# Keeping a group's split weights in DRAM, and finer-grained row splits, in a fused attention, MoE and feed-forward kernel

## The chip, the cores and the metric

The kernel runs on one core of a Trainium2 chip. The metric is the device time of one execution in microseconds. Before the change the median of 3 runs is 956.89 us (955.63 to 957.21).

## The reference

Three layers in float32, 1,792 rows of 768. Sigmoid attention over 4 x 12 heads, a mixture of 8 experts of which each row uses its best one, and a dense gated feed-forward layer. The change lies in the last:

```python
def _moe2_ref(x, w_gate, w_val, w_out):          # 1792 x 768, 768 x 1536 (twice), 1536 x 768
    gate = 1.0 / (1.0 + np.exp(-(x @ w_gate)))
    val = x @ w_val
    return (gate * val @ w_out).astype(np.float32)
```

## The kernel before, in words

Attention comes first, then the experts (to about 468 us), then the feed-forward layer. Only the last is described.

It works in two row blocks, sb = 0 and 1, of 896 rows, and each in two stages. `gv_stage` (L1517) makes gate times value in 12 groups g: 6 tiles of features, for each a gate group (g even) and a value group (g odd). A group is one Strassen-Winograd product of 2 x 2 blocks: 7 products of sums of weight blocks and sums of row blocks. `o_stage` (L1655) multiplies by w_out the same way, 7 products for each of 3 (block 0) or 4 (block 1) pairs of row tiles.

For TensorE (PE) each operand x is split: hi = x rounded to fp32r, lo = x - hi, and a product is hi·hi + lo·hi + hi·lo: in `product` (L1420) three matmuls for each of 3 slices, so 9 matmuls of 128 x 448 in `gv_stage`, and 18 of 128 x 384 in `o_stage`. The hi part is a cast on ScalarE (ACT), the lo part a subtraction on VectorE (DVE).

- Rows: `y_load` brings a tile of expert output (yd, in DRAM) by a DMA from POOL; `y_turn` (L1303) transposes it on PE and copies it into YB. `y_sum` makes T1 to T4, `y_split` (L1356) splits a block. The lo part of B11, B21, B22 or T1 (`yl`) takes the place of that block itself in YB.
- Weights: `ff_load` fetches a group's raw blocks from wd by a DMA from SP into one of three buffers wr. `w_sums` (L1401, DVE, four instructions) makes S1 to S4; `w_hi` (ACT, L1413) and `w_lo` (DVE, L1418) split in two halves: blocks 0 to 2 (1152 columns) and 3 to 6 (1536 columns), into `wh` (two buffers, in turn) and `wl` (in place of wr).
- Some raw weights lie packed in DRAM and are unpacked by `decode` (DVE, L236 to L242, three steps).
- Output stage: `t_split` splits w_out's blocks (th, tl), loaded by `o_load` into q; `s_prep` (L1616) splits the squares of gate times value (sr).

PE's program order within a group is the order of the products; `gv_first` starts the next group's A11·B11 before this group's last two products. All other work is placed by hand between products: behind product n of a group, `hooks(n)` issues work on ACT, DVE and SP (n = 0 to 3 behind the first four, 4 behind `gv_first` of the next group, 5 and 6 behind S4·B22 and A22·T4). In `o_stage` `o_hooks(n, j)` does so behind product n of pair j. Each engine runs its instructions in the order of issue, so an instruction that waits holds everything behind it on that engine. Results leave PSUM by `out(k, ...)` on DVE (gate groups: t0g; value groups: G) and by copies on ACT: s, u (t0u, t1u), v (t0v, t1v). An operand's name tells block and part: y0B22hi is block 0, B22, hi part.

```python
        for n, f in enumerate(((p6, p2, p5, p7) if sb else (p6, p7, p5, p2)) if last else
                              (p2, p7, p6, p5) if (sb, g) == (1, 0) else (p7, p6, p2, p5)):
            f()
            if n < 3:
                hooks(n)
        out(3, d, u4)
        hooks(3)
```

The last two row tiles of the output leave by a direct DMA on SP, the others by an indirect one on POOL (`store`, L1646).

## Time and profile before

| | us |
|---|---|
| median of 3 runs | 956.89 |
| the profiled execution | 956.68 |
| its span | 954.6 |
| PE busy | 928.1 (97%) |
| DVE busy | 737.4 (77%) |
| ACT busy | 544.8 (57%) |
| POOL busy | 147.9 (15%) |
| feed-forward part, first matmul of block 0 | 468.69 |
| first matmul of block 1 | 702.88 |
| end of the last sum on DVE | 950.84 |

Matmuls are pipelined: a row of the timeline gives a matmul's start and its duration, and one begins every 0.20 us (128 x 448) or 0.17 us (128 x 384) while each lasts 0.36 or 0.33. In square brackets stands the time that the engine sat idle before, and the operation that ended it. SPq and POOLq are DMA issues. PEclk is the granted clock of PE as a share of its higher level.

### The profile page before, as it was taken

How to read it: one execution, taken by the hardware profiler on the slowest of the kernel's cores; microseconds unless marked ns; L12 is line 12 of the kernel's file. 1: busy time of each engine (PE TensorE's matmuls, PEld its weight loads, DVE VectorE, ACT ScalarE, POOL GpSimd, SP SyncE). 2: the span in 40 equal slices, each digit the busy share in tenths (PEclk: the TensorE clock that was granted, in tenths of full speed). 3: DMA queues.
4: the chain of work that ended last, by engine and by line, in shares of the span. 5: the costliest groups of instructions: out<-in, count | busy, mean ns of one | idle time of the engine just before them, and what ended most of it. 6: DMA issues, size and time to landing. Idle time of an engine off the chain costs nothing.

```text
span 954.6 us, 14878 instructions
## 1 busy us (share of the span) xinstructions
PE 928.1 (97%) x5757; PEld 781.6 (82%) x5757; DVE 737.4 (77%) x912; ACT 544.8 (57%) x645; POOL 147.9 (15%) x124
## 2 busy tenths in 40 slices
PE   9999999998999999999999999989999999999998
PEld 4555556887887887889978999989988999999998
DVE  6867767988998876799959888676997666658674
ACT  6586766576766666779643344355664343445451
POOL 0011112233052222324400000000220000000011
PEclk9999999999999999999989999999999999999999
DMA  8999967455899998766406554264231111125112
GB/s 300 336 341 340 331 209 276 155 179 186 301 406 420 313 331 336 260 238 199 149 1 215 181 173 159 94 251 152 83 116 67 56 47 65 67 100 199 50 50 83
DMA packets 36974, 186.40 MB, mean 195 GB/s; under 512 B 4680, under 2 KB 6744, under 8 KB 32800
## 3 DMA queue, kind: packets, MB, share of 16 engines
q1 hardware_dynamic: 25680, 134.29, 40.1%
q0 software_dynamic: 11216, 51.09, 14.2%
q8 instruction: 46, 0.75, 0.3%
q14 instruction: 32, 0.26, 0.1%
HBM read 180.94 MB, written 35.88 MB: 227 GB/s over the span
## 4 chain that ended last, share of the span: by engine, by line
PE 68%; DMA 2%; DVE 2%; ACT 2%; issue 1%; ACTq 0%; DVEq 0%
PE pb L1424 15%; PE pb L1425 15%; PE pb L1423 15%; PE h L1104 8%; PE y L1088 3%; PE y L1090 3%; PE y L1089 3%; DMA Y<-yd 2%; PE qh L1193 2%; PE qy L1216 1%; PE hTp L1123 1%; DMA yd<-yo,ridx 1%; PE xTp L950 1%; DVE tl L1586 1%; PE yTp L1313 1%
## 5 line engine op out<-in xcount | busy, mean ns | idle before, releaser
L281 DVE TENSOR_TENSOR rg<-raw,rg 128x1536 fp32r<-128x1536 f32 x104 | 179.9, 1752 | 32.0 <-ACT rg L280 26.6
L280 ACT CAST rg<-raw 128x1536 fp32r<-128x1536 f32 x102 | 150.4, 1480 | 59.1 <-PE y L1089 29.0
L1424 PE MATMUL pb<-yl,wh 128*128 128x448 f32 x288 | 105.7, 367 | 2.2 <-DVE yl L1359 2.2
L1104 PE MATMUL h<-rg,xh 128*128 128x512 f32 x336 | 102.2, 398 | 0.3 <-ACT rg L280 0.3
L1425 PE MATMUL pb<-th,sr 128*128 128x384 f32 x294 | 98.4, 335 | 1.4 <-DVE sr L1625 1.4
L1423 PE MATMUL pb<-th,sr 128*128 128x384 f32 x294 | 98.9, 336 | 0.0
L1424 PE MATMUL pb<-tl,sr 128*128 128x384 f32 x294 | 98.4, 335 | 0.2 <-DVE tl L1586 0.2
L436 ACT ACTIVATE attn<-sc,bias_s 128x896 f32<-128x896 f32 x84 | 79.1, 1004 | 28.3 <-PE sc L434 28.0
L1418 DVE TENSOR_TENSOR wl<-wr,wh 128x1536 fp32r<-128x1536 f32 (+1 forms) x43 | 67.9, 1580 | 16.1 <-ACT wh L1413 13.7
L1104 PEld LDWEIGHTS h<-rg,xh 128*128 128x128 f32 x336 | 61.2, 188 | 15.1 <-issue 1.6
L448 PE MATMUL av<-attn,v 128*64 128x448 f32 (+1 forms) x384 | 70.6, 545 | 0.6 <-DVE xT L453 0.5
L1088 PE MATMUL y<-rg,hh 128*128 128x384 f32 x192 | 67.1, 349 | 1.5 <-DVEq L1247 1.5
L1413 ACT CAST wh<-wr 128x1536 fp32r<-128x1536 f32 (+1 forms) x43 | 57.3, 1333 | 18.4 <-PE pb L1424 14.3
L1090 PE MATMUL y<-rg,hh 128*128 128x384 f32 x192 | 65.4, 341 | 1.2 <-DVE rg L281 1.2
L1089 PE MATMUL y<-rg,hl 128*128 128x384 f32 x192 | 65.4, 341 | 0.9 <-DVE hl L1129 0.8
L1104 PE MATMUL h<-rg,xl 128*128 128x512 f32 x168 | 61.5, 393 | 0.0
L1424 PEld LDWEIGHTS pb<-yl,wh 128*128 128x128 f32 x288 | 54.2, 188 | 7.3 <-DVE yl L1359 3.0
L1652 POOL DMA_INDIRECT out<-o,idc x12 | 17.5, 1458 | 271.4 <-ACT o L1670 227.6
L1425 PEld LDWEIGHTS pb<-th,sr 128*128 128x128 f32 x294 | 55.2, 188 | 1.7 <-DVE sr L1625 1.7
L1424 PEld LDWEIGHTS pb<-tl,sr 128*128 128x128 f32 x294 | 55.2, 188 | 0.6 <-DVE tl L1586 0.6
L1423 PEld LDWEIGHTS pb<-th,sr 128*128 128x128 f32 x294 | 55.2, 188 | 0.0
L1623 ACT CAST sr<-G 128x768 fp32r<-128x768 f32 x42 | 35.1, 838 | 30.4 <-PE pb L1424 18.9
(499 smaller groups left out, 2108.3 us busy)
## 6 DMA issues: line engine op xcount, KB each, us to landing
raw<-in_w1P SPq DMA_DIRECT2D x52, 768.0 KB
raw<-in_w2P SPq DMA_DIRECT2D x52, 768.0 KB
q<-wob SPq DMA_DIRECT2D x14, 1152.0 KB
wr<-wd SPq DMA_DIRECT2D x19, 768.0 KB
sg<-in_wffP SPq DMA_DIRECT2D x9, 1536.0 KB
kq<-in_kqP SPq DMA_DIRECT2D x24, 448.0 KB
stg<-in_wffP SPq DMA_DIRECT2D x5, 1536.0 KB
Y<-yd POOLq DMA_DIRECT2D x14, 384.0 KB, 6.5
```

The lines of the kernel that those rows point to most:

```text
L280: (hi_eng.tensor_copy if hi_eng else A.copy)(hi, raw)
L281: V.tensor_sub(lo, raw, hi)
L436: A.activation(at_, ps[:, :, :S], AF.Sigmoid, bias=bias_s, scale=1.0 / math.sqrt(HD))
L448: T.matmul(av_t[j * HD : (j + 1) * HD, i % 2, :S], v[rows, j * HD : (j + 1) * HD], at_[rows, j, :], start=(u == first_unit(i)), stop=(u == ...
L1088: T.matmul(o, ah[:, ks], bh[:, w], start=(k == 0), stop=False)
L1089: T.matmul(o, al[:, ks], bh[:, w], start=False, stop=False)
L1090: T.matmul(o, ah[:, ks], bl[:, w], start=False, stop=(k == nk - 1))
L1104: T.matmul(ps[:, half, :], x[:, k * P : (k + 1) * P], w[:, s * 512 : (s + 1) * 512], start=(k == 0 and x is xh and w is hi), stop=(k == KD ...
L1418: V.tensor_sub(w_los(g, half), raw, w_his(sb, g, half))
L1423: T.matmul(o, ah[:, k], bh[:, k], start=(first and k == 0), stop=False, skip_group_check=open_)
L1424: T.matmul(o, ah[:, k], bl[:, k], start=False, stop=False, skip_group_check=open_)
L1425: T.matmul(o, al[:, k], bh[:, k], start=False, stop=(k == n - 1), skip_group_check=open_)
```

## The change

1. A buffer `wkeep` in DRAM. The split weights of group (0, 0) go there by four DMAs from POOL (`w_keep`); block 1 fetches them with four DMAs from SP (`w_kept`) in place of loading raw weights, summing and splitting them again. Their hi part lies in a buffer of its own (`whk`).
2. YB becomes four buffers, yb00 to yb11. A turned tile is copied in two instructions everywhere.
3. In the first group of both blocks the casts of B22 and T4 stand at hooks 0 and 1, their subtractions at hooks 1 and 2 (before: both at 3 and 4). T1 of block 1 is split at hook 0 (before 1), T2 of block 0 one step earlier.
4. The scaling of the last expert pair stands earlier, in two halves.
5. The list of PSUM banks is rotated by two.
6. Block 1's first group runs p2, p6, p7, p5. `out(3)` follows as soon as p5 and p7 are both done.
7. In the second group the unpacking stands at hooks 2, 4, 6 (before 4, 5, 6). In block 1 `s_prep(1, 0)` stands at hook 2 of the last group (before 5). The first two turns of rows in block 0's output stage come one product later: (0, 2) and (1, 0).
8. The last row tile's store goes in two halves.

```diff
-    def y_split(sb, name):
+    def y_split(sb, name, parts=(0, 1)):
         hi, lo = buf(f"y{sb}{name}hi", y_place(sb, name + "hi"), KH, TH, dt=F32R), y_lo(sb, name)
-        A.copy(hi, y_raw(sb, name))
-        V.tensor_sub(lo, y_raw(sb, name), hi)
+        if 0 in parts:
+            A.copy(hi, y_raw(sb, name))
+        if 1 in parts:
+            V.tensor_sub(lo, y_raw(sb, name), hi)
...
     def y_block(kh, th):
-        return YB[:, kh, th]
+        return buf(f"yb{kh}{th}", (SB_Y, (2 * kh + th) * YA), KH, TH)
...
+    def w_keep():
+        for half, (a, b) in enumerate(HALVES):
+            for k, z in enumerate((w_his(0, 0, half), w_los(0, half))):
+                G.dma_start(wkeep[:, k, a * YW : b * YW], z.bitcast(U32))
+
+    def w_kept(half, ks=(0, 1)):
+        a, b = HALVES[half]
+        for k in ks:
+            z = w_los(0, half) if k else w_his(1, 0, half)
+            SP.dma_start(z.bitcast(U32), wkeep[:, k, a * YW : b * YW])
...
+        elif (sb, g) == (1, 0):
+            products = (p2, p6, p7, p5)
+        done = []
+        for n, f in enumerate(products):
             f()
-            if n < 3:
-                hooks(n)
-        out(3, d, u4)
-        hooks(3)
+            done.append(f)
+            if f in (p5, p7) and p5 in done and p7 in done:
+                out(3, d, u4)
+            hooks(n)
...
                 if g == 0:
-                    y = {1: sb and "T1", 3: "B22", 4: "T4"}.get(at_)
-                    if y:
-                        y_split(sb, y)
+                    if at_ == 0 and sb:
+                        y_split(sb, "T1")
+                    if at_ < 2:
+                        y_split(sb, ("B22", "T4")[at_], (0,))
...
+                    if g == 0 and at_ in (1, 2):
+                        y_split(sb, ("B22", "T4")[at_ - 1], (1,))
...
+                    if at_ == 5 - 3 * sb:
+                        s_prep(sb, 0)
                     if at_ - 1 - 2 * sb in (0, 1):
                         t_split(sb, 0, at_ - 1 - 2 * sb)
-                    elif at_ == 5:
-                        s_prep(sb, 0)
...
-                if dec is not None and at_ >= 4:
-                    decode(dec, at_ - 4)
+                when = (2, 4, 6) if g == 1 else (4, 5, 6)
+                if dec is not None and at_ in when:
+                    decode(dec, when.index(at_))
...
-                    if n in (4, 6):
+                    if sb and j == 3 and n > 4:
+                        h = int(n == 5)
+                        SP.dma_start(out[N - P :, h * 384 : (h + 1) * 384], o[:, h])
+                    elif n in (4, 6):
                         store(sb, q if n == 4 else r, o)
...
-    O_TURNS = {(0, 1): 0, (0, 2): 1, (1, 1): 2, (1, 2): 3, (2, 0): 4, (2, 1): 5, (2, 2): 6}
+    O_TURNS = {(0, 2): 0, (1, 0): 1, (1, 1): 2, (1, 2): 3, (2, 0): 4, (2, 1): 5, (2, 2): 6}
...
         if (n, j) == (4, 2):
-            ff_load(0)
+            w_kept(0)
+            w_kept(1, (1,))
         elif (n, j) == (5, 2):
             ff_load(1)
             ff_load(2)
-            w_sums(1, 0, 0)
         elif (n, j) == (6, 0):
             y_split(1, "B11")
-            w_sums(1, 0, 1)
         elif (n, j) == (6, 1):
-            w_hi(1, 0, 0)
-            w_lo(1, 0, 0)
+            w_kept(1, (0,))
             y_split(1, "B21")
         elif (n, j) == (6, 2):
             y_split(1, "T3")
-            w_hi(1, 0, 1)
-            w_lo(1, 0, 1)
...
+        if c == NW2 - 1:
+            y_scale(NSTAT - 1, 2)
         ff_first(c)
+    w_keep()
...
-    one_bank += [pbp.tile([P, 512], F32, name=f"pb{i}") for i in range(8)]
+    banks = [pbp.tile([P, 512], F32, name=f"pb{i}") for i in range(8)]
+    one_bank += banks[2:] + banks[:2]
```

ACT at the start of block 0, before, from the copy t0s of group 0 (wh is the next group's weights, t0g a gate):

```order
L1448 COPY t0s<-pb_6095 128x448
L1413 CAST wh_6129<-wr_5880 128x1152
L1483 COPY t0u_6114<-pb_6095 128x448
L1491 COPY t0v<-pb_6095 128x448
L1465 ACTIVATE t0g_6116<-t0g_6116 128x448
L1358 CAST y0B22hi<-YB 128x1344
L1413 CAST wh_6129<-wr_5880 128x1536
L1465 ACTIVATE t0g_6119<-t0g_6119 128x448
L1448 COPY t0s<-pb_6096 128x448
L1358 CAST y0T4hi<-y0T_5763 128x1344
```

The same place in the changed kernel:

```order
L1464 COPY t0s<-pb_6114 128x448
L1360 CAST y0B22hi<-yb_5456 128x1344
L1418 CAST wh_6149<-wr_5892 128x1152
L1499 COPY t0u_6131<-pb_6114 128x448
L1360 CAST y0T4hi<-y0T_5775 128x1344
L1507 COPY t0v<-pb_6114 128x448
L1481 ACTIVATE t0g_6133<-t0g_6133 128x448
L1418 CAST wh_6149<-wr_5892 128x1536
```

The casts of B22 and T4 have moved ahead of the copies t0u and t0v, which wait for products of PE.

DVE at the start of block 1, before, from the first sum o of the last pair (o are sums of the output stage, L1405 to L1409 weight sums, wl weight splits):

```order
L1672 TENSOR_TENSOR o_1_7303<-pb_6100,U_7245 128x384
L1359 TENSOR_TENSOR y1T3lo<-y1T_7495,y1T3hi 128x1344
L1418 TENSOR_TENSOR wl_1_6066<-wr_5878,wh_6045 128x1536
L1359 TENSOR_TENSOR y1T2lo<-y1T_7570,y1T2hi 128x1344
L1464 TENSOR_TENSOR t1g_7763<-pb_6097,t1s 128x448
L1405 TENSOR_TENSOR wr_5880<-wr_5880 128x384
L1406 TENSOR_TENSOR wr_5880<-wr_5880 128x384
L1359 TENSOR_TENSOR yl_5938<-YB,y1T1hi 128x1344
L1408 TENSOR_TENSOR wr_5880<-wr_5880 128x384
L1409 TENSOR_TENSOR wr_5880<-wr_5880 128x384
L1418 TENSOR_TENSOR wl_0_6145<-wr_5880,wh_6129 128x1152
L1464 TENSOR_TENSOR t1g_7766<-pb_6099,t1v 128x448
```

In the changed kernel:

```order
L1698 TENSOR_TENSOR o_1_7321<-pb_6119,U_7254 128x384
L1362 TENSOR_TENSOR y1T3lo<-y1T_7513,y1T3hi 128x1344
L1362 TENSOR_TENSOR y1T2lo<-y1T_7588,y1T2hi 128x1344
L1480 TENSOR_TENSOR t1g_7776<-pb_6116,t1s 128x448
L1362 TENSOR_TENSOR yl_5950<-yb_5454,y1T1hi 128x1344
L1410 TENSOR_TENSOR wr_5892<-wr_5892 128x384
L1411 TENSOR_TENSOR wr_5892<-wr_5892 128x384
L1413 TENSOR_TENSOR wr_5892<-wr_5892 128x384
L1414 TENSOR_TENSOR wr_5892<-wr_5892 128x384
L1423 TENSOR_TENSOR wl_0_6168<-wr_5892,wh_6149 128x1152
L1362 TENSOR_TENSOR yl_6147<-yb_5456,y1B22hi 128x1344
L1362 TENSOR_TENSOR y1T4lo<-y1T_7640,y1T4hi 128x1344
```

The weight split wl_1 of group 0 is gone from between T3 and T2 (the other half and the sums, earlier, too), and B22 and T4 stand ahead of the gate sum that waits for t1v.

SP's queue at the end of block 0's output stage, before the change only loads of raw weights, with it:

```order
L1601 DMA q_7176<-wob_78 128x2304
L1434 DMA wh_7612<-wkeep 128x1152
L1434 DMA wl_0_6059<-wkeep 128x1152
L1434 DMA wl_1_6082<-wkeep 128x1536
L1324 DMA wr_5892<-wd_65 128x1536
L1324 DMA wr_6061<-wd_66 128x1536
L1434 DMA wh_6239<-wkeep 128x1536
L1324 DMA wr_5890<-wd_67 128x1536
```

Three loads of kept parts stand where one raw load (of wd_64) stood, and the fourth behind the raw loads of groups 1 and 2.

## Rows read from the trace of the kernel before

**Rows 1.** The page, busy time of each engine.

```profile
PE 928.1 (97%) x5757; PEld 781.6 (82%) x5757; DVE 737.4 (77%) x912; ACT 544.8 (57%) x645; POOL 147.9 (15%) x124
```

**Rows 2.** Timeline of PE, block 0's first two groups: start, duration, operation.

```profile
477.97 0.36 PE L1423 MATMUL pb<-y0B11hi,wh 128*128 128x448 f32 x1
...
480.49 0.47 PE L1423 MATMUL pb<-y0B22hi,wh 128*128 128x448 f32 x1 [0.53 <-ACT y0B22hi L1358]
...
491.14 0.36 PE L1423 MATMUL pb<-y0T2hi,wh 128*128 128x448 f32 x1
...
492.96 0.36 PE L1423 MATMUL pb<-y0B21hi,wh 128*128 128x448 f32 x1
```

**Rows 3.** Stretch table there: busy time by engine, PEclk, DMA share, GB/s.

```profile
485.00:490.00 5.00, 4.43 (x12) 3.96 (x13) 3.22 (x4) 0.49 (x2) 0.00 (x0) 0.50 0.00 0
```

**Rows 4.** Timeline of ACT and DVE there.

```profile
478.22 0.53 ACT L1491 COPY t0v<-pb 128x448 f32<-128x448 f32 x1 [3.17 <-PE pb L1425]
...
479.13 1.31 ACT L1358 CAST y0B22hi<-YB 128x1344 fp32r<-128x1344 f32 x1
...
480.47 1.56 DVE L1359 TENSOR_TENSOR yl<-YB,y0B22hi 128x1344 fp32r<-128x1344 f32 x1 [1.06 <-ACT y0B22hi L1358]
```

**Rows 5.** Timeline of DVE, ACT and PE, block 0's second and third group.

```profile
497.43 0.62 DVE L1469 TENSOR_TENSOR G<-pb,t0v 128x448 f32<-128x448 f32 x1 [1.16 <-ACT t0v L1491]
...
500.49 0.95 DVE L236 TENSOR_SCALAR spare<-stg 128x1536 uint32<-128x1536 uint32 x1
...
506.91 1.16 ACT L1413 CAST wh<-spare 128x1152 fp32r<-128x1152 f32 x1 [7.70 <-DVE spare L242]
...
507.35 0.37 PE L1425 MATMUL pb<-y0B21hi,wl 128*128 128x448 f32 x1
508.55 0.47 PE L1423 MATMUL pb<-y0T1hi,wh 128*128 128x448 f32 x1 [0.82 <-ACT t0u L1483]
```

**Rows 6.** Timeline of DVE and PE, block 0's last group.

```profile
625.44 1.36 DVE L1586 TENSOR_TENSOR tl<-q,th 128x1152 fp32r<-128x1152 f32 x1 [2.09 <-ACT th L1585]
...
628.58 0.47 PE L1423 MATMUL pb<-y0T4hi,wh 128*128 128x448 f32 x1 [1.20 <-DVE G L1469]
```

**Rows 7.** Timeline of POOL and PE, first turned rows in block 0's output stage.

```profile
630.79 1.07 POOL L1301 DMA_DIRECT2D Y<-yd  x2 [33.62 <-PE pb L1425]
...
638.22 0.88 PE L1313 MATMUL pb<-cs,Y 128*128 128x128 f32 x6 [1.27 <-DMA Y<-yd]
```

**Rows 8.** Timeline of PE, block 1's first group.

```profile
702.88 0.36 PE L1423 MATMUL pb<-y1B11hi,wh 128*128 128x448 f32 x1
...
711.04 0.48 PE L1423 MATMUL pb<-y1T1hi,wh 128*128 128x448 f32 x1 [0.62 <-ACT t1u L1483]
...
717.22 0.47 PE L1424 MATMUL pb<-yl,wh 128*128 128x448 f32 x1 [1.12 <-DVE yl L1359]
...
722.43 0.37 PE L1423 MATMUL pb<-y1T3hi,wh 128*128 128x448 f32 x1
```

**Rows 9.** Timeline of DVE there.

```profile
703.17 0.55 DVE L1672 TENSOR_TENSOR o<-pb,U 128x384 f32<-128x384 f32 x1
...
705.10 1.75 DVE L1418 TENSOR_TENSOR wl<-wr,wh 128x1536 fp32r<-128x1536 f32 x1
...
711.30 0.55 DVE L1408 TENSOR_TENSOR wr<-wr 128x384 f32<-128x384 f32 x1
```

**Rows 10.** Timeline of SP's queue, end of block 0's output stage.

```profile
694.76 0.80 SPq L1323 DMA_DIRECT2D wr<-wd  x2
```

**Rows 11.** Stretch table there, last column GB/s.

```profile
702.00:704.00 2.00, 2.00 (x13) 1.91 (x12) 2.00 (x3) 2.00 (x2) 1.17 (x1) 1.00 0.00 0
```

**Rows 12.** Timeline of PE, start of block 1's output stage.

```profile
862.96 0.44 PE L1425 MATMUL pb<-th,sr 128*128 128x384 f32 x1 [1.39 <-DVE sr L1625]
```

**Rows 13.** Timeline of DVE, the last sum.

```profile
950.28 0.56 DVE L1672 TENSOR_TENSOR o<-pb,U 128x384 f32<-128x384 f32 x1 [2.57 <-PE pb L1425]
```

**Rows 14.** Stretch table at the end.

```profile
952.00:953.00 1.00, 0.00 (x0) 0.00 (x0) 0.00 (x0) 0.00 (x0) 0.00 (x0) 1.00 0.73 298
```

More of the change, by code (lines that the diff above doesn't have):

```diff
@@ L168, in routed_kernel @@
     wd = [drp.tile([P, CH], F32, name=f"wd{k}") for k in range(KF2)]
+    wkeep = drp.tile([P, 2, GW], U32, name="wkeep")
     wob = [drp.tile([P, 4, WQ], F32, name=f"wob{k}") for k in range(2)]
@@ L1146, in routed_kernel, with y_scale @@
     yo_t = {}
-    def y_scale(p):
+    def y_scale(p, parts=1):
         yo_t[p] = mp.tile([P, 2, 384], F32, tag="yo", name=f"yo{p}")
-        A.activation(yo_t[p], yp_t.pop(p)[:, :, :384], AF.Copy, scale=gate_s[:, p : p + 1])
+        y = yp_t.pop(p)
+        for a in range(2) if parts == 2 else (slice(None),):
+            A.activation(yo_t[p][:, a], y[:, a, :384], AF.Copy, scale=gate_s[:, p : p + 1])
     def y_out(p):
@@ L1315, in y_turn @@
             n0, n1 = max(q * P, th * TH), min(q * P + P, (th + 1) * TH)
-            if n0 < n1 and t < SB // P:
-                A.copy(YB[:, :, th, :, n0 - th * TH : n1 - th * TH], z[:, :, :, n0 - q * P : n1 - q * P])
-            elif n0 < n1:
+            if n0 < n1:
                 for kh in range(2):
-                    A.copy(YB[:, kh, th, :, n0 - th * TH : n1 - th * TH], ps[kh][:, :, n0 - q * P : n1 - q * P])
+                    A.copy(y_block(kh, th)[:, :, n0 - th * TH : n1 - th * TH], ps[kh][:, :, n0 - q * P : n1 - q * P])
     def ff_load(c):
@@ L1388, in w_his @@
             return buf("wh00", (SB_RAW, 8 * YA), b * YW, dt=F32R)
+        if (sb, g) == (0, 0):
+            return buf("whk", SB_RT, GW, dt=F32R)[:, a * YW : b * YW]
         return buf(f"wh{g % 2}", (SB_RING, g % 2 * GW), GW, dt=F32R)[:, a * YW : b * YW]
@@ L1494, in gv_group @@
         last = g + 1 == NG
-        for n, f in enumerate(((p6, p2, p5, p7) if sb else (p6, p7, p5, p2)) if last else (p2, p7, p6, p5) if (sb, g) == (1, 0) else (p7, p6, p2, p5)):
-            f()
-            if n < 3:
-                hooks(n)
-        out(3, d, u4)
-        hooks(3)
+        products = (p7, p6, p2, p5)
+        if last:
+            products = (p6, p2, p5, p7) if sb else (p6, p7, p5, p2)
+        elif (sb, g) == (1, 0):
+            products = (p2, p6, p7, p5)
+        done = []
+        for n, f in enumerate(products):
+            f()
+            done.append(f)
+            if f in (p5, p7) and p5 in done and p7 in done:
+                out(3, d, u4)
+            hooks(n)
         gates()
@@ L1534, in hooks @@
                         w_lo(sb, g + 1, 0)
-                    elif at_ == 3:
+                    if g == 0 and at_ in (1, 2):
+                        y_split(sb, ("B22", "T4")[at_ - 1], (1,))
+                    if at_ == 3:
                         w_hi(sb, g + 1, 1)
@@ L1539, in hooks @@
                 else:
+                    if at_ == 5 - 3 * sb:
+                        s_prep(sb, 0)
                     if at_ - 1 - 2 * sb in (0, 1):
                         t_split(sb, 0, at_ - 1 - 2 * sb)
-                    elif at_ == 5:
-                        s_prep(sb, 0)
-                    elif at_ == 6:
+                    if at_ == 6:
                         s_prep(sb, 1)
                         s_prep(sb, 2)
-                if dec is not None and at_ >= 4:
-                    decode(dec, at_ - 4)
+                when = (2, 4, 6) if g == 1 else (4, 5, 6)
+                if dec is not None and at_ in when:
+                    decode(dec, when.index(at_))
                     if at_ == 6 and dec != DIRECT[-1]:
@@ L1721, in ff_first @@
         elif c == 2:
+            y_split(0, "T2")
             w_hi(0, 0, 1)
@@ L1724, in ff_first @@
         else:
-            y_split(0, "T2")
             y_split(0, "B21")
@@ L1745, in routed_kernel @@
         f()
-    YB = buf("YB", SB_Y, 2, 2, KH, TH)
     Y2 = buf("Y2", SB_Y2, 2, D)
```

## Prediction

> **What bounds the kernel now.** I read the page first: TensorE (PE) is busy 928.1 of 954.6 us [rows 1], and no other engine comes near, so the time can only fall where PE stands still or runs slowly. There are 26.5 us of that. The change touches nothing before the last pair of routed tiles, so I then listed PE's rows in the feed-forward part alone (the timeline of PE, from 468 us to the end) and looked for matmuls that begin much more than 0.2 us after the one before. An unhindered product of nine matmuls takes 492.96 - 491.14 = 1.82 us [rows 2]; every stretch below is held against a multiple of it. The reader is to see that the losses are few and large, and that each has one named operation of ACT, DVE or a DMA at its end. A stop costs PE a little more than the idle time printed: in the third group of products 0.82 us of idle stand between matmuls that begin 508.55 - 507.35 = 1.20 us apart, where 0.20 is usual, so 1.0 is lost [rows 5]. I add 0.2 to an idle time for that.
>
> **The change, term by term.**
>
> *Start of row block 0.* From the A11·B11 product of group 1 to the product p6 of that group PE takes 491.14 - 477.97 = 13.17 us [rows 2]. Four products are 4 x 1.82 = 7.3, so 5.87 us are lost. The first stop waits for ACT's cast of B22 [rows 2]. That cast begins at 479.13, although B22 had been in place for long: in program order it stands behind the copy t0v, which ACT waited 3.17 us for PE to make possible [rows 4]. DVE's low part can only follow (480.47 plus 1.56) [rows 4], and T4 comes after both. And the stops have a second price: in 485 to 490 us the granted clock is 0.50, the lower of the two levels, and only 12 matmuls run in 5 us, where 25 would [rows 3]; just before, PE had stood waiting. The change casts B22 and T4 behind products 0 and 1 and subtracts behind 1 and 2. Counted forward by the durations of rows 4, on engines that are idle there, B22 is split by about 477.4 and T4 by about 479.4; they are needed at about 480.0 and 481.8. No stop, so no slow stretch. Term: -5.9. Bounds: -4 if another 1.9 us stop (one cast and the copies before it) remains, -5.9 if none does.
>
> *Third group (g = 2), p5.* ACT sat 7.70 us on the cast of raw weights that DVE's unpacking was still to deliver; the copy t0u that PE needs stood behind it in the queue [rows 5]. The change starts unpacking two hooks earlier, in a place where DVE idles 1.16 us; the first of its three steps takes 0.95 [rows 5], so the chain behind it ends about 0.95 earlier. The stop of 1.0 goes nearly whole. Term: -1.0, bounds 0 and -1.1. It is 0 if the earlier step only pushes an eviction back.
>
> *Last group of block 0.* PE waits 1.20 us before its T4 product for DVE's sum for output block 3, which had stood behind the weight split tl (1.36) and the two instructions of output block 0 [rows 6]. Done before both, it is in time. What is late next is the split of the first square of the output stage, which DVE now does as close to its use as before; the same split in block 1 makes PE wait 1.39 [rows 12]. So of 1.20 + 0.2 I count half, -0.7, with bounds 0 and -1.4.
>
> *First transposed rows in the output stage.* The load of rows Y is issued at 630.79, both tiles at once, and PE takes them at 638.22 after 1.27 us of idle [rows 7]: 7.4 us, behind other loads. Moving that turn one product of 3.1 us later covers it. Term: -1.4 (1.27 + 0.2, less a little). The next turns keep their places and their load is issued a product later, so up to 1.4 can come back: bounds 0 and -1.5.
>
> *Start of row block 1.* From the first product to the second group's p7 PE takes 722.43 - 702.88 = 19.55 us [rows 8], where eight products are 14.6: 4.95 lost, in stops for ACT's t1u and, largest, for the low parts of B22 (1.12) [rows 8] and T4. The change removes here four weight sums, two casts and two subtractions: on DVE 4 x 0.55 for the sums and some 1.4 and 1.75 for the subtractions [rows 9], 5.3 us of a queue that had no gaps, and on ACT two casts of the size of the 1.16 one in rows 5 and somewhat above. It also sets p7 between p6 and p5, so that copying t1u has a product's time. In the new order DVE's chain from 703.17 [rows 9] is: o, T3 low, T2 low, a gate sum, T1 low, four sums, a weight split, B22 low, T4 low, at about 1.5 us for each low part [rows 4]. T2 low ends near 706.6, where its product's second matmul starts at 702.88 + 2 x 1.82 + 0.2 = 706.7; the weight split ends near 712.1, where it is wanted at 702.88 + 5 x 1.82 + 0.2 = 712.2; T4 low ends near 715.1 and the sum that frees the bank near 715.7, where the T4 product starts at 715.6. Everything fits with next to nothing over, so I leave 0.5 us lost. Term: -4.4.
>
> Its risk is the reload. Three of the four kept pieces come some 20 us ahead. The fourth, 768 KB, waits for PE's product two before the block's end, about 699.8, on a queue behind two more 768 KB loads. Those were issued at 694.76 in the kernel before [rows 10], and no data moves any more in 702 to 704 us [rows 11]: at most 7.2 us for both. The piece is wanted at 702.88 + 2 x 1.82 = 706.5. Lower end: half of 7.2 after its issue, 703.4, in time. Upper end: 7.2 for it alone, 707.0, which is 0.5 late; and if the loads before it are late by their own half, 3.6, it is 4.1 late. I take the lower end, since the row shows two loads in that time. The Trainium skill, "DMA: Bandwidth & Descriptors", section "Anatomy of one DMA — SWDGE (gpsimd) path", gives a transfer a fixed 2.0 us, most of it the receipt of the last write, plus its bytes at 436 GB/s: by that the piece would take 3.8 us (an estimate), land at 703.6, and the sum would stay; that rule is for another issuing path than SP's, and no row here shows such a load alone.
>
> *Output stage of block 1.* PE waits 1.39 us for DVE's split of the first square [rows 12]; the change does this three hooks (over 5 us) earlier. Term: -1.6, bounds 0 and -1.6.
>
> *End.* After the last sum on DVE (950.28 + 0.56 = 950.84) 3.76 us pass to the span's end [rows 13]. The last store carries half as much. Bounds: 0 if the rest is fixed, -1.9 if it all scales. In 952 to 953 us the engines move 298 GB/s with 0.73 of them busy [rows 14], so 408 at full share: 196.6 KB fewer save 0.48. Term: -0.45.
>
> *At nothing.* The four writes of kept weights go out on POOL, of which no other work is due but a store that nobody reads for 150 us; if that were late, rows of block 1 would be late too. The seven more ACT copies in the routed part stand under PE's matmuls there. T2's cast moves forward by one step, and the scaling in halves adds one short instruction. The separate row buffers take away false waits of one block's low part for another's; they cost no time of any engine. Cover gone, each would cost under 1 us.
>
> **Sum.** 5.9 + 1.0 + 0.7 + 1.4 + 4.4 + 1.6 + 0.45 = 15.45. The profiled execution took 956.68 (span 954.6 and 2.1 around it), so 941.2; it stands 0.2 below the median of the runs, 956.89, and against that I say 941.4.
>
> **The rivals.**
> - *Late reload.* The fourth piece lands up to 4.1 us late, as above, or the turns of rows wait again. For it: DMA queues are busy up to 702 [rows 10, 11]. Against it: three quarters of the data is early. It gives 942.5 to 946.
> - *The waits move.* Block starts are full to the last half microsecond by my own count, so a sum or a copy that comes 1 us late at each of five places (both block starts, p5, both output stages), with half of block 0's slow-clock stretch staying, gives back 5 to 8 us: 946 to 950. For it: DVE was the last releaser in most groups [rows 6, 8, 12]. Against it: 5.3 us of DVE work disappears.
> - *Nothing gained.* Operations are set earlier in program order, but still wait for data or buffers that come at the old time (the split row blocks share their place with their low parts). Then the stops stay where they are: 955 to 958.5. Against it: B22 stood ready in rows 4, it was the queue that held it.
> - *Slower.* One mechanism: the banks are rotated, and if each of the 168 products of both blocks then began its first matmul late behind a copy of the same bank, the price is 168 times that delay. Above 15.45 / 168 = 0.092 us it eats all; at 0.12 the time is 961. For it: a stop does spread over the first matmuls [rows 5]. Against it: the list is shifted as a whole, so the distance between a bank's uses stays the same.
>
> **How the numbers follow.** My forecast, all terms within 3 us (938.5 to 943.5): 0.62. Late reload: 0.17. Waits move: 0.14. Nothing gained: 0.04. Slower: 0.03. About 0.2% (1.9 us) is what a measurement of this kernel tells from no change. The first three cases are all faster by more: 0.93; same 0.04, slower 0.03. The range takes the forecast and the late reload whole and the nearer edge of the third: 938.5 to 947.
>
> **What would show it.** In the new trace: no PE stop over 0.3 us and a granted clock of 1.00 between 475 and 495; no ACT wait before p5 of the third group; less than 1 us before the last T4 product of block 0; the first turn without a DMA behind it; eight products at the start of block 1 in about 15 us; no wait for sr at the start of the last stage; a tail of about 3.3 us after the last sum. PE's busy time should fall by about 3 us only, where the clock was low; the rest comes from idle. I am wrong if a kept piece releases PE in block 1, if the clock drops elsewhere, or if PE's stops come back behind DVE.

## The result, and the profile after

The changed kernel takes 945.86 us (median of 4 runs, 944.22 to 950.01); the kernel before, run beside it, 957.05 (955.63 to 958.31). The ratio is 0.989 (95% interval 0.9853 to 0.9927): 11 us faster, against 15.45 forecast. The profiled execution took 944.67, its span is 942.6, so 12.0 below the span of before.

The page of the changed kernel, busy time:

```profile
PE 926.7 (98%) x5757; PEld 781.3 (83%) x5757; DVE 733.1 (78%) x906; ACT 542.5 (58%) x652; POOL 148.5 (16%) x128
```

PE's busy time fell by only 1.4, not by the 3 that the slow-clock stretch alone would have given: something in it has grown. The stages tell where. Timeline of PE and DVE, the first row of each stage and the last sum, first of the kernel before:

```profile
468.69 0.36 PE L1423 MATMUL pb<-y0B11hi,wh 128*128 128x448 f32 x1
630.54 0.34 PE L1423 MATMUL pb<-th,sr 128*128 128x384 f32 x1
861.06 0.33 PE L1423 MATMUL pb<-th,sr 128*128 128x384 f32 x1
```

(702.88 and 950.28 stand in [rows 8, 13]) and of the changed one, with the experts' last matmul ahead:

```profile
468.49 0.34 PE L1091 MATMUL y<-rg,hh_last 128*128 128x384 f32 x1
469.97 0.47 PE L1439 MATMUL pb<-y0B11hi,whk 128*128 128x448 f32 x1 [1.14 <-ACT yo L1153]
626.16 0.36 PE L1439 MATMUL pb<-th,sr 128*128 128x384 f32 x1
697.82 0.36 PE L1439 MATMUL pb<-y1B11hi,wh 128*128 128x448 f32 x1
851.42 0.34 PE L1439 MATMUL pb<-th,sr 128*128 128x384 f32 x1
939.07 0.56 DVE L1698 TENSOR_TENSOR o<-pb,U 128x384 f32<-128x384 f32 x1 [2.57 <-PE pb L1441]
```

| stretch | before | after | difference | forecast |
|---|---|---|---|---|
| up to block 0's first product | 468.69 | 469.97 | +1.28 | 0 |
| block 0, gate times value | 161.85 | 156.19 | -5.66 | -7.6 |
| block 0, output | 72.34 | 71.66 | -0.68 | -1.4 |
| block 1, gate times value | 158.18 | 153.60 | -4.58 | -4.4 |
| block 1, output, to the last sum | 89.22 | 87.65 | -1.57 | -1.6 |
| from there to the span's end | 4.32 | 3.53 | -0.79 | -0.45 |
| sum | 954.6 | 942.6 | -12.0 | -15.45 |

The last three forecasts hold or are passed, the first three miss 3.9 us together. Two things there were not in the forecast. The first is the wait in the second row above: ACT's scaling of the last expert pair, which PE did not wait for before. The second shows in no wait at all. Timeline of PE of the changed kernel, one product of block 0 and the next:

```profile
486.66 0.37 PE L1439 MATMUL pb<-y0T2hi,wh 128*128 128x448 f32 x1
488.52 0.37 PE L1439 MATMUL pb<-y0B21hi,wh 128*128 128x448 f32 x1
```

A product takes 1.86 us here; before it took 1.82 [rows 2], at the same place. The matmuls begin 0.207 us apart in place of 0.203, from the second group to the end of the stage (in the first group 0.2045), while nothing is waited for and PEclk is 1.00. The stretch table of the changed kernel, for 475 to 490 us (before, the last of these stood at 0.50 [rows 3]):

```profile
475.00:480.00 5.00, 5.00 (x26) 4.61 (x25) 4.78 (x4) 2.22 (x4) 0.14 (x1) 1.00 0.58 239
480.00:485.00 5.00, 5.00 (x26) 4.60 (x25) 2.38 (x2) 3.35 (x6) 0.00 (x0) 1.00 0.00 0
485.00:490.00 5.00, 5.00 (x26) 4.54 (x26) 3.94 (x6) 2.16 (x3) 0.00 (x0) 1.00 0.00 0
```

PE's 84 products of block 0, 1.824 us each at the old spacing, make 153.2 us; the stage took 156.2 without a single stop over 0.25 us. So 2.9 us are the spacing's. All stops that the forecast named in that stage are gone, with the slow stretch 5.9 + 1.1 + 1.5 by the starts of the matmuls, and 2.9 came back.

### The profile page after: what moved, and what is told of

Read it like the earlier page. It is cut to its first block, busy times and chain, and to the rows that moved or that the text cites. A ratio compares the mean times of both kernels' runs of the same rounds, so it can differ in the third digit from the quotient of the medians.

```text
span 942.6 us, 14905 instructions
## 1 busy us (share of the span) xinstructions
PE 926.7 (98%) x5757; PEld 781.3 (83%) x5757; DVE 733.1 (78%) x906; ACT 542.5 (58%) x652; POOL 148.5 (16%) x128
## 4 chain that ended last, share of the span: by engine, by line
PE 74%; DVE 1%; ACT 1%; issue 0%; DVEq 0%; ACTq 0%
PE pb L1441 16%; PE pb L1440 16%; PE pb L1439 16%; PE h L1105 9%; PE y L1089 3%; PE y L1091 3%; PE y L1090 3%; PE qh L1196 2%; PE qy L1219 2%; PE hTp L1124 1%; PE xTp L951 1%; PE yTp L1316 1%; PE pb L1316 0%; DVE tl L1612 0%; ACT rg L281 0%
## 5 line engine op out<-in xcount | busy, mean ns | idle before, releaser
L1440 PE MATMUL pb<-yl,wh 128*128 128x448 f32 x276 | 101.3, 367 | 0.0
L1423 DVE TENSOR_TENSOR wl<-wr,wh 128x1536 fp32r<-128x1536 f32 (+1 forms) x39 | 61.8, 1584 | 15.9 <-ACT wh L1418 13.6
L1418 ACT CAST wh<-wr 128x1536 fp32r<-128x1536 f32 (+1 forms) x39 | 52.0, 1333 | 14.3 <-PE pb L1440 14.3
L1440 PEld LDWEIGHTS pb<-yl,wh 128*128 128x128 f32 x276 | 51.9, 188 | 4.6
```

The lines of the kernel that those rows point to most:

```text
L1423: V.tensor_sub(w_los(g, half), raw, w_his(sb, g, half))
L1440: T.matmul(o, ah[:, k], bl[:, k], start=False, stop=False, skip_group_check=open_)
```

## The experiments

Times are medians; each set of runs has its own runs of the kernel before beside it (957.98 us for e1 to e4, 956.74 for e5 to e8, 958.63 for e9 and e10, 956.6 for e11, 957.15 for e12). "Stage" is the time from a stage's first matmul to the next stage's.

**e1_tick: one matmul added.** Is the spacing a pattern that any disturbance resets?

```diff
             gv_group(sb, g, hooks)
+            if sb == 0 and g == 0:
+                T.matmul(one_bank[7][:, :64], w_op(0, 1, A11)[0][:, 0],
+                         yop["B11"][0][:, 0, :64], start=True, stop=True)
```

> The changed kernel with one PE matmul of 64 columns added behind the first group of block 0, into a PSUM bank that nobody reads; nothing else differs. In the changed kernel's profile the matmuls of block 0 begin every 0.207 us, from the first group to the last, where the kernel before has 0.203 (both at a granted clock of 1.00); at the start of block 1 both kernels begin with 0.207 and fall to 0.203 behind the first small hitch of a weight load. Theory 1, a pattern that PE keeps until something disturbs it: behind the added matmul the spacing is 0.203, block 0's first stage (156.2 us) falls by 2.7 to 3.0, the time by as much. Theory 2, something that block 0 of the changed kernel has all along (its buffers, its rotated banks, its DMAs): the spacing stays 0.207, the time rises by 0.1.

944.5 us (943.27 to 946.51). Block 0's stage took 155.59, 0.6 less than the changed kernel's. Before the added matmul, in this run, the spacing lay between, at about 0.204; with the first matmul behind it (485.9 us) it was 0.203; at 518.8 us, where nothing had been added and no stop is shown, it went over to 0.207 and stayed there. So the buffers and banks of block 0 do not force 0.207 on it, and what the added matmul sets can be lost again: theory 1 by half.

**e2_banks: banks not rotated.**

```diff
-    one_bank += banks[2:] + banks[:2]
+    one_bank += banks
```

> The changed kernel with the list of PSUM banks not rotated. In the changed kernel's profile PE waits 1.14 us before block 0's first product for ACT's scaling of the last expert pair, which the kernel before does not. Theory 1, the rotated list gives the first product one of the banks from which ACT still scales: that wait goes, 1.2 to 1.3 us. Theory 2, the wait is for something else, or the next product takes it over in the unrotated list: 0 to 0.5. If the rotated banks are also what makes matmuls begin every 0.207 us in block 0, the spacing is 0.203 here and another 2.9 us go; if it is a pattern kept by chance, nothing says which of the two it will be here.

943.57 us (942.26 to 945.15). Timeline of PE, the last matmul of the experts and the first product:

```profile
467.57 0.34 PE L1091 MATMUL y<-rg,hh_last 128*128 128x384 f32 x1
467.75 0.37 PE L1439 MATMUL pb<-y0B11hi,whk 128*128 128x448 f32 x1
```

The wait is gone and nothing takes it over: theory 1. From the experts' last matmul to the first product 1.48 us pass in the changed kernel and 0.18 here, so rotating the list, with the scaling where the change put it, costs 1.3 us; what it would cost with the scaling in its old place, no run shows. The spacing in block 0 was 0.207 here too (stage 156.09), so it does not need the rotated banks.

**e3_split: B22 and T4 split late again.**

```diff
-                    if at_ < 2:
-                        y_split(sb, ("B22", "T4")[at_], (0,))
+                    if at_ in (3, 4):
+                        y_split(sb, ("B22", "T4")[at_ - 3])
...
-                    if g == 0 and at_ in (1, 2):
-                        y_split(sb, ("B22", "T4")[at_ - 1], (1,))
```

> The changed kernel with the splits of B22 and T4 back where they were, casts and subtractions both at hooks 3 and 4, in both blocks. Theory 1 (the prediction's): block 0 again has stops for B22 and T4 and a stretch at half clock, 5 to 6 us lost at its start; if a disturbed pattern also means 0.203 us spacing behind it, 2.7 us come back over the rest of block 0, so that the time rises by 3 only. In block 1, with kept weights, DVE has room, so stops of 1 us at most. Theory 2, the row blocks' own buffers had already freed the splits: no stops, time as the changed kernel's within 0.5.

955.72 us (950.82 to 960.35, 10 runs), nearly the time of before. In its profile (950.4 span) the stops of block 0 are back, timeline of PE:

```profile
482.37 0.47 PE L1439 MATMUL pb<-y0B22hi,whk 128*128 128x448 f32 x1 [0.50 <-ACT y0B22hi L1360]
483.96 0.47 PE L1440 MATMUL pb<-yl,whk 128*128 128x448 f32 x1 [1.12 <-DVE yl L1362]
487.45 0.47 PE L1440 MATMUL pb<-y0T4lo,whk 128*128 128x448 f32 x1 [1.12 <-DVE y0T4lo L1362]
```

but its clock did not fall. Stretch table:

```profile
480.00:485.00 5.00, 3.37 (x16) 2.52 (x15) 2.18 (x2) 4.89 (x7) 0.00 (x0) 1.00 0.00 0
485.00:490.00 5.00, 3.87 (x18) 3.00 (x17) 3.85 (x4) 1.35 (x2) 0.00 (x0) 1.00 0.00 0
```

Block 0's stage took 159.98, 3.8 more than the changed kernel's, and block 1's 157.07, 3.5 more, so the earlier splits work in both blocks. Block 0 lost less than the 5 to 6 expected, since the clock stayed, and the spacing behind the stops was 0.207; stops of at most 1 us in block 1 were too low a forecast. The medians lie further apart, by 9.9 us, than the profiles (7.8); where the rest goes, no profile shows. The slow clock is not bound to these stops in every execution: of the ten timed runs six have a mean granted clock of 0.993 and three 0.996, as the profiled one has; no timed run of e1, e2 and e8, which have no such stops, has less than 0.996. So the lower clock seems to come with the stops in part of the executions, and the profile of before was one of these; where it fell in those six is not shown. The mean clock does not sort the times either: the fastest of the ten (950.82) has 0.993.

**e4_nokeep: no kept weights.**

```diff
-    w_keep()
...
-            w_kept(0)
-            w_kept(1, (1,))
+            ff_load(0)
...
             ff_load(2)
+            w_sums(1, 0, 0)
         elif (n, j) == (6, 0):
             y_split(1, "B11")
+            w_sums(1, 0, 1)
         elif (n, j) == (6, 1):
-            w_kept(1, (0,))
+            w_hi(1, 0, 0)
+            w_lo(1, 0, 0)
             y_split(1, "B21")
         elif (n, j) == (6, 2):
             y_split(1, "T3")
+            w_hi(1, 0, 1)
+            w_lo(1, 0, 1)
```

> The changed kernel without the kept weights: block 1 loads group 0's raw weights, sums and splits them as the kernel before did, with all other parts of the change in place. Theory 1 (the prediction's): DVE has 5.3 us more ahead of block 1's first products and falls behind, PE loses 2 to 4.5 us there. Theory 2, the earlier splits, the order p2, p6, p7, p5 and T1's place do it all: 0 to 0.5 us lost, and the kept weights bring nothing.

947.0 us (946.21 to 948.85). One stop returns, timeline of PE:

```profile
703.54 0.47 PE L1440 MATMUL pb<-y1T2lo,wh 128*128 128x448 f32 x1 [1.41 <-DVE y1T2lo L1362]
```

Block 1's stage took 154.98, 1.4 more than the changed kernel's. Between the theories: the kept weights, the change's largest part in code, bring 1.4 of the 4.6 us at block 1's start; order, splits and buffers bring the rest.

**e5_four: four parts undone, each read at its own place.**

```diff
-                when = (2, 4, 6) if g == 1 else (4, 5, 6)
+                when = (4, 5, 6)
...
-    O_TURNS = {(0, 2): 0, (1, 0): 1,
+    O_TURNS = {(0, 1): 0, (0, 2): 1,
...
-                    if at_ == 5 - 3 * sb:
+                    if at_ == 5:
...
-                    if sb and j == 3 and n > 4:
+                    if False:
```

> The changed kernel with four separate parts undone at once, since each can be read at its own place in the trace: unpacking in the second group at hooks 4, 5, 6 again; the first two turns of rows at (0, 1) and (0, 2) again; the first split of squares in block 1 at hook 5 again; the last store whole. The prediction's prices: a stop of about 1.0 before the third group's p5, one of 1.3 to 1.4 before the first turn, one of 1.4 to 1.6 at the start of the last stage, and a tail longer by 0.45; in all 4.2 to 4.5. Rival: the other parts alone have given these places room (the row copies' own buffers, the earlier splits), then some of the four stops do not return, and the sum is under 2.5.

948.45 us (945.25 to 955.83, 10 runs). Timeline of PE, POOL and DVE:

```profile
506.79 0.47 PE L1439 MATMUL pb<-y0T1hi,wh 128*128 128x448 f32 x1 [0.62 <-ACT t0u L1499]
627.55 1.08 POOL L1304 DMA_DIRECT2D Y<-yd  x2 [32.12 <-PE pb L1441]
628.30 0.44 PE L1441 MATMUL pb<-th,sr 128*128 128x384 f32 x1 [0.38 <-DVE sr L1651]
634.68 0.55 PE L1316 MATMUL pb<-cs,Y 128*128 128x128 f32 x3 [0.21 <-DMA Y<-yd]
854.92 0.44 PE L1441 MATMUL pb<-th,sr 128*128 128x384 f32 x1 [1.39 <-DVE sr L1651]
942.25 0.56 DVE L1698 TENSOR_TENSOR o<-pb,U 128x384 f32<-128x384 f32 x1 [2.57 <-PE pb L1441]
```

The unpacking's stop is back with 0.62 of idle (0.8 by the starts of the matmuls), the first turn's with 0.21 only (0.4), the first square's with 1.39 (1.55), and the tail is 946.4 - 942.25 = 4.15, 0.62 longer. In all 3.4, between the two expectations. The later turn hardly matters here: PE came to the rows 0.75 us later in the stage than before the change, most of it for the stop of 0.38 in front, and they were there 7.1 us after their issue, where the kernel before took 7.4 [rows 7]. Block 0's spacing was 0.207 up to 507 us and 0.203 behind the stop there.

**e6_order: old order in block 1's first group, output 3 behind the fourth product.**

```diff
-            products = (p2, p6, p7, p5)
+            products = (p2, p7, p6, p5)
...
-            if f in (p5, p7) and p5 in done and p7 in done:
+            if n == 3:
                 out(3, d, u4)
```

> The changed kernel with the old order of products in block 1's first group (p2, p7, p6, p5) and with output 3 taken always behind the fourth product. Prediction's prices: 1.4 to 1.5 before the T4 product of block 0's last group, and 0.8 to 1.0 before p5 in block 1's first group (for the copy t1u); 2.2 to 2.5 in all. Rival: DVE has had so much taken off in block 0's last group and block 1 that neither wait returns; under 0.5. The spacing of matmuls in block 0 may be 0.203 or 0.207 us here; 2.9 us hang on that alone and are told apart by it.

947.61 us (947.14 to 947.85). Both waits return, timeline of PE:

```profile
627.46 0.47 PE L1439 MATMUL pb<-y0T4hi,wh 128*128 128x448 f32 x1 [1.13 <-DVE G L1485]
708.77 0.47 PE L1439 MATMUL pb<-y1T1hi,wh 128*128 128x448 f32 x1 [0.62 <-ACT t1u L1499]
```

Block 0's first stage has 157.56 (+1.4), block 1's 154.24 (+0.6); the stage between has 0.5 less, since the first split of squares is then in time. So the two waits cost 2.0, a little under the 2.2 to 2.5 expected, and 1.5 net.

**e7_hooks: the kernel before with the earlier splits alone.**

```diff
-                    y = {1: sb and "T1", 3: "B22", 4: "T4"}.get(at_)
-                    if y:
-                        y_split(sb, y)
+                    if at_ == 0 and sb:
+                        y_split(sb, "T1")
+                    if at_ < 2:
+                        y_split(sb, ("B22", "T4")[at_], (0,))
...
+                    if g == 0 and at_ in (1, 2):
+                        y_split(sb, ("B22", "T4")[at_ - 1], (1,))
```

> The kernel before with one part of the change alone: casts of B22 and T4 at hooks 0 and 1, subtractions at 1 and 2, T1 of block 1 at hook 0; YB stays one buffer, nothing is kept. Theory 1 (the prediction's): this alone removes the stops at block 0's start and whatever slow clock follows them: 3.1 to 5.9 less than before there. In block 1 DVE has no room without the kept weights, so that what the earlier splits give is lost again before T2 or the weights: less than 2 gained. Theory 2, without buffers of their own the casts and subtractions wait for one another's blocks in YB: under 1.5 gained in block 0.

953.04 us (950.8 to 957.76, 10 runs), 3.7 below before. Block 0's stage fell from 161.85 to 156.26, so this part alone earns the forecast's -5.9 there (5.6). Block 1's rose to 159.13, with one long stop. Timeline of DVE, ACT and PE:

```profile
704.16 1.55 DVE L1361 TENSOR_TENSOR yl<-YB,y1T1hi 128x1344 fp32r<-128x1344 f32 x1
705.75 1.31 ACT L1359 CAST y1B22hi<-YB 128x1344 fp32r<-128x1344 f32 x1 [3.67 <-DVE yl L1361]
709.23 0.52 ACT L1485 COPY t1u<-pb 128x448 f32<-128x448 f32 x1
709.80 0.69 PE L1425 MATMUL pb<-y1T1hi,wh 128*128 128x448 f32 x1 [3.99 <-ACT t1u L1485]
```

And behind that stop the clock fell, stretch table:

```profile
710.00:715.00 5.00, 5.00 (x18) 4.50 (x19) 3.06 (x3) 1.51 (x3) 0.00 (x0) 0.67 0.00 0
```

ACT's cast of B22 waits 3.67 us for a subtraction that writes another block of YB (the low part of T1), with the copy that PE wants behind it. So theory 1 holds in block 0; in block 1, where it left up to 2 us of gain, 1 us was lost, by the kind of wait that theory 2 had expected in block 0.

**e11_own: e7_hooks with the row blocks' own buffers** (and, with them, a turned tile copied in two instructions). It asks whether that wait is a false one.

```diff
     def y_block(kh, th):
-        return YB[:, kh, th]
+        return buf(f"yb{kh}{th}", (SB_Y, (2 * kh + th) * YA), KH, TH)
```

> The kernel before with two parts of the change: the earlier splits of e7_hooks and the row blocks' own buffers; no kept weights, old order of products. In e7_hooks PE waited 3.99 us before block 1's first p5 for the copy t1u, which stood on ACT behind the cast of B22, which waited 3.67 us for DVE's low part of another block of YB. Theory 1, that wait is a false one of the single buffer YB: ACT's wait goes, PE's stop for t1u falls to 0.6 to 0.8 (which the order of products leaves), with a stop of up to 1.6 for T2's low part, and block 1's first stage (159.1 us) takes 155 to 157 with the spacing at 0.203. Theory 2, it is DVE's work that is late, whatever the buffers: a stop of 3 us or more stays there.

950.19 us (946.72 to 952.71), 6.4 below before. The cast now starts without a wait and the copy t1u waits for PE alone. Timeline of ACT and PE:

```profile
699.74 1.31 ACT L1357 CAST y1B22hi<-yb 128x1344 fp32r<-128x1344 f32 x1
703.62 0.53 ACT L1483 COPY t1u<-pb 128x448 f32<-128x448 f32 x1 [0.28 <-PE pb L1425]
704.20 0.48 PE L1423 MATMUL pb<-y1T1hi,wh 128*128 128x448 f32 x1 [0.62 <-ACT t1u L1483]
```

Block 1's stage took 154.99, the low edge of the 155 to 157 expected, without the stop for T2's low part that was allowed for. Theory 1: the single buffer made the wait, and the earlier splits pay in block 1 only with buffers of their own.

**e8_ticks: banks not rotated, and a 64-column matmul behind each of block 0's first eleven groups** (as in e1, for every g below 11).

> The changed kernel with banks not rotated, and a 64-column matmul that nobody reads behind each of block 0's first eleven groups (0.1 us each). What is asked is what makes the spacing of matmuls 0.203 or 0.207 us. Theory 1, any small disturbance of the weight loads draws the spacing anew: in block 0 groups of either spacing stand side by side, and the stage takes 1 to 2 us less than with 0.207 throughout, before the 1.1 us that the added matmuls cost. Theory 2, something of block 0 holds the spacing at 0.207 (with the one added matmul it was 0.203 before it and up to the fourth group, then 0.207): all groups but the first few have 0.207.

943.43 us (941.43 to 944.79). The spacing in block 0 lay at 0.2045 before the first added matmul and at 0.203 from it (483.4 us) to the stage's end, which took 154.53 with the eleven additions. It did not go to and fro, so "draws anew" is wrong; each addition leaves 0.203. And block 1, where nothing was added, had 0.207 from 708 to its end, 156.37 us.

**e9_best and e10_changed: the best version, and the changed kernel again.** e9 has the banks not rotated and block 0's first split of squares a hook earlier:

```diff
-    one_bank += banks[2:] + banks[:2]
+    one_bank += banks
...
-                    if at_ == 5 - 3 * sb:
+                    if at_ == 4 - 2 * sb:
```

> The changed kernel with the banks not rotated, and with the first split of squares of block 0 at hook 4 of its last group instead of 5 (it was 0.37 us late for PE in the changed kernel). Expected: the 1.14 us wait before block 0's first product and the wait for the split both go, 1.5 to 1.8 us less than the changed kernel beside it, if the spacing of matmuls in block 0 is the same in both; with the spacing at 0.203 instead of 0.207, 2.9 less still. Rival: the earlier split pushes an eviction back that PE waits for, then the 0.4 stays or grows.

> The changed kernel again, as a reference on the same chip. Theory (spacing drawn by chance at small hitches): the two spacings need not fall as in its first profile, where block 0 had 0.207 and block 1 0.203; the times spread over some 3 to 6 us between executions, in steps of about 3. Rival (spacing fixed by the program): the same spacing in the same blocks as in the first profile.

e9 took 943.4 us (941.81 to 945.33), e10 945.57 (944.88 to 945.91) on the same chip. The wait before block 0 is gone in e9. The 0.38 wait for the squares stayed: ACT's cast ahead of the split starts only as DVE's product of gate and value ends (624.88 plus 0.63), whatever its place in the order. Timeline of ACT and DVE of e9:

```profile
624.88 0.63 DVE L1486 TENSOR_TENSOR G<-G,t0g 128x448 f32<-128x448 f32 x1
625.54 0.83 ACT L1649 CAST sr<-G 128x768 fp32r<-128x768 f32 x1 [2.76 <-DVE G L1486]
626.41 0.96 DVE L1651 TENSOR_TENSOR sr<-G,sr 128x768 fp32r<-128x768 f32 x1 [0.90 <-ACT sr L1649]
```

So e9 gains about 2.2 by the medians, of which 1.3 are accounted for, and its ratio to the kernel before is 0.9838 (0.9816 to 0.9861). e10 decides on the spacing in block 1. Timeline of PE, the first row of block 1's first stage and of the next:

```profile
696.49 0.36 PE L1439 MATMUL pb<-y1B11hi,wh 128*128 128x448 f32 x1
852.85 0.34 PE L1439 MATMUL pb<-th,sr 128*128 128x384 f32 x1
```

156.36 us, where the same kernel's first profile has 851.42 - 697.82 = 153.60, neither with a stop over 0.25 us in it. In block 1 the spacing is not fixed by the program; it differs from execution to execution. In block 0 it was 0.207 again from the second group on, as in every profile of the changed kernel and its variants without an added matmul (e2, e3, e4, e6, e9; in e5 up to its stop), so there something in the program may favour it; what, no run shows. All four timed runs lie within 1.1 us: the expected spread of 3 to 6 us, in steps of 3, did not show.

**e12_hold: the added matmul in both blocks,** behind every second group, banks not rotated.

> The changed kernel with banks not rotated, and the 64-column matmul behind every second group of both blocks (six in each, 0.1 us each). In e1_tick and e8_ticks the spacing went to 0.203 with the very matmul that follows the first added one; in e1_tick it lapsed to 0.207 some 33 us later, with none added in between, in e8_ticks (one every 13 us) it never lapsed in block 0, and in block 1, with none, it did. Theory 1, an added matmul sets the spacing to 0.203 each time, and it lapses by chance: both blocks have 0.203 but for stretches of under 26 us that end at an added matmul; block 0's stage takes 154 to 155, block 1's 154 to 154.5, the times lie together, 941 to 943. Theory 2, what followed the two first ones was chance: stretches of 0.207 run on across added matmuls, stages of 156 to 157 occur.

943.43 us (941.4 to 944.46). Timeline of PE in block 0, the first matmul of each product around the first addition (the one of 64 columns):

```profile
482.55 0.37 PE L1439 MATMUL pb<-y0B22hi,whk 128*128 128x448 f32 x1
...
484.39 0.36 PE L1439 MATMUL pb<-y0T4hi,whk 128*128 128x448 f32 x1
...
486.23 0.19 PE L1588 MATMUL pb<-y0B11hi,wh 128*128 128x64 f32 x1
486.26 0.44 PE L1439 MATMUL pb<-y0T3hi,wh 128*128 128x448 f32 x1
...
488.16 0.36 PE L1439 MATMUL pb<-y0T2hi,wh 128*128 128x448 f32 x1
```

Two products of 1.84 stand ahead of it, as all from the stage's start. Behind it, once the addition is paid for, a matmul begins every 0.203 us, so 1.82 a product, to the end of the stage. In block 1 the longer spacing came up at 707.0 us and had ended at 710.5, before the addition at 712.10:

```profile
710.48 0.36 PE L1440 MATMUL pb<-y1T4lo,wh 128*128 128x448 f32 x1
712.10 0.19 PE L1588 MATMUL pb<-y1B11hi,wh 128*128 128x64 f32 x1
```

Eight matmuls begin in the 1.62 us between these two, 0.2025 each. A longer spacing did not come up again in either block. The stages took 154.07 and 154.25, as theory 1 had it and against theory 2; but no later lapse came up for an added matmul to end, and the times did not lie together at 941 to 943. Six additions of 0.11 each are the price, 0.7 a block, so that against e9 (156.09 and 153.60) the two stages together gain 1.4, which the medians, equal to 0.1, do not show.

## Why the prediction was right, and where it was off

The direction and the range held, and the stops that it named went: the time lies 1.1 us inside the upper edge of the range, and 4.5 above the forecast value. It lies outside the forecast's own band (938.5 to 943.5) and is in the range only through the band of the late reload, which did not happen; that part is luck. By its own steps:

- *Start of block 0, -5.9.* Right, and due to the earlier splits alone (e7: 5.6). The bound of -4 was the better guide to a typical execution without the slow clock: e3 lost 3.8 there at a clock of 1.00. I took the slow stretch for a fixed price of the stops; it is one that some executions pay.
- *p5 of the third group, -1.0.* e5 has 0.8. *Last group, -0.7.* The stop of 1.5 went whole; the split of squares that I named as next was late by 0.37 idle, about 0.6 with its aftermath (0.5 by e6), so 0.8 to 0.9 net.
- *First turn, -1.4.* The stop is gone, but undoing this part costs only 0.4 (e5): a later start of the turn and an earlier landing of its rows had nearly removed it.
- *Start of block 1, -4.4.* Measured -4.6: the eight products take 14.98 us in place of 19.55 [rows 8], and 15.00 in e10, though its whole stage fell by only 1.8 for the longer spacing. The share was misjudged: I rested the term on DVE's 5.3 us, and the kept weights are worth 1.4 (e4). The earlier splits are worth 3.5 (e3), and they need the separate buffers, which I had put under "At nothing" with a cover of under 1 us; from e7 to e11 block 1's stage falls by 4.1 (159.13 to 154.99), a slow stretch in e7 included.
- *The reload* was in time. It was issued at 694.89, and the product that wants it began at 701.53 without a wait:

```profile
694.89 0.32 SPq L1434 DMA_DIRECT2D wh<-wkeep  x1
701.53 0.36 PE L1439 MATMUL pb<-y1T2hi,wh 128*128 128x448 f32 x1
```

- *Output stage of block 1, -1.6:* 1.57. *End, -0.45:* 0.79, of which e5 gives 0.62 to the halved store. By the rule of the Trainium skill ("DMA: Bandwidth & Descriptors", section "Anatomy of one DMA — SWDGE (gpsimd) path"), which is for another issuing path than SP's, 196.6 KB fewer would save 0.45, an estimate; e5 shows 0.17 more than that.
- *The step that failed* is the rotated banks. I dismissed them with "the list is shifted as a whole, so the distance between a bank's uses stays the same", which is true between products, but not for the first use behind the experts: +1.28 in the table, of which e2 takes back 1.3. The second miss is the assumption that an unhindered product takes 1.82 us; here it took 1.86 for most of 84 products, +2.9. The trace of the kernel before could have warned of it: its first two products of block 1 start 1.86 apart (702.88 [rows 8], 704.74, 706.60), at a clock of 1.00 [rows 11] and with no wait:

```profile
704.74 0.37 PE L1423 MATMUL pb<-y1B21hi,wh 128*128 128x448 f32 x1
706.60 0.37 PE L1423 MATMUL pb<-y1T3hi,wh 128*128 128x448 f32 x1
```

- *What that adds up to.* The two misses make 4.2 together, more than the 3.5 between forecast and profile: the stops of block 0's first stage gave 0.9 more than forecast (8.5 for 7.6), the end 0.3, block 1's start 0.2, and block 0's output stage 0.7 less.

None of the rivals is what happened as it was written: no reload was late; of "The waits move" only the split of squares came late, at one place (0.37 us); and of "Slower" a product did wait behind the last use of its bank, but once, for 1.3 us, and not at each of 168 products.

## What to carry to other kernels

Where an engine works in order, look at what stands ahead of the late instruction before looking at how long it takes: two casts and their subtractions, moved ahead of copies that wait for PE, were worth more (3.8 and 3.5 us, e3) than removing 5.3 us of DVE work (1.4, e4). Cutting a buffer into pieces that are written and read apart can matter as much as the order, since a subtraction into one block held a cast of another for 3.7 us. When a list of PSUM banks is renumbered, follow the first use of each bank back to the last use by the stage before.

## What the runs showed of the hardware

Matmuls of 128 x 448 that wait for nothing settle at 0.203 or at 0.207 us from one start to the next, at a granted clock of 1.00 in both cases, and keep to it for up to 150 us: 2.8 us for a stage of 84 products. In the first group of block 0 the mean lay between, at 0.2045. The same kernel had both in the same stage (block 1, e10). Where a matmul of 64 columns stood at the border behind block 0's first group, the spacing behind it was 0.203 (three profiles of three: e1, e8, e12); without it and without a stop ahead it was 0.207 from that border on in all six such profiles of the changed kernel and its variants (its own, e2, e4, e6, e9, e10). The stop of 0.62 us in e5 brought 0.203 too. Other changes to 0.207 came where a new group's first product starts, or near it (518.8 us in e1, 707 in e12). Why one or the other is kept stays open: the weight loads take 0.19 us in both. Stops do not bring the shorter one every time: behind the three of e3 in block 0 it was 0.207.

Short stops of PE bring the lower clock in some executions and not in others. After stops of 0.50, 1.12 and 1.12 us it stayed at 1.00 in the profile of e3. In the profile of before it had fallen after the first two, of 0.53 [rows 2] and 1.12 us, and was 0.50 in 485 to 490 us [rows 3]. Timeline of PE and stretch table of before:

```profile
482.08 0.47 PE L1424 MATMUL pb<-yl,wh 128*128 128x448 f32 x1 [1.12 <-DVE yl L1359]
483.00:485.00 2.00, 1.90 (x6) 1.17 (x4) 1.05 (x1) 1.35 (x2) 0.00 (x0) 0.55 0.00 0
```
